# A sparse-attention and mixture kernel: the mixed tile goes to the end of a pair, value products and inverse spreads get fixed tiles, and the steps within a tile stand in another order

## The chip, the cores and the metric

The kernel runs on one core of a Trainium2 chip. The core has five engines with instruction streams of their own: TensorE (PE, with its weight loads shown apart as PEld), VectorE (DVE), ScalarE (ACT), GpSimd (POOL) and SyncE (SP), which issues the transfers. Each works through its stream in the order written; between the streams only semaphores set an order. The metric is the device time of one execution in microseconds (us); less is better.

## The reference

Attention with a threshold, then two feed-forward parts. Cut to the core:

```python
def _attn_ref(q, k, v, tau):             # q, k, v: (4, 8, 576, 64)
    scores = scale * np.matmul(q, k.transpose(0, 1, 3, 2))
    thresh = np.max(scores, axis=-1, keepdims=True) - tau
    scores = np.where(scores >= thresh, scores, -1000000000.0)
    scores = scores - np.max(scores, axis=-1, keepdims=True)
    attn = np.exp(scores)
    attn = attn / (np.sum(attn, axis=-1, keepdims=True) + 1e-09)
    return np.matmul(attn, v)
...
x = attn_out.transpose(0, 2, 1, 3).reshape(B * S, H * D)   # 2304 x 512
x = ((x @ w1) * (x @ w2)) @ w3 @ w_out
...  # gates P by 8 rounds of row and column scaling, then 8 experts:
for e in range(E):
    out += P[:, e:e + 1] * (np.maximum(x @ w1[e], 0.0) @ w2[e])
```

## The kernel before

The 32 heads are taken as 16 pairs. A pair has 9 tiles of 128 query rows: four of each head, and one **mixed tile** that holds the last 64 rows of both heads. TILES gives their order within a pair; the mixed tile `(None, 4)` stands fifth. Tiles are counted through from 0 to 143 (s), and the main loop of `attention` runs once for each s; below, t is s within its pair (0 to 8), and "step s" is one turn of the loop.

A tile goes through these operations, most of them spread over several turns:

- `scores` (PE, L158): four products of 288 columns, high and low part of k, into one of two PSUM buffers `s`. The mixed tile needs eight. Turn s makes the scores of tile s + 2.
- `rowmax` (DVE, L163), `thresh` and `expo` (ACT, L166, L171), also for tile s + 2 in turn s.
- `mask` (DVE, L178), for tile s in turn s: it compares with the threshold, multiplies and sums, and with its end the buffer `s` of that tile is free. As there are two buffers, the scores of tile s + 2 wait for the mask of tile s.
- `transp` (PE, L203) and `evac` (ACT, L208), for tile s - 1: four transposes into the only PSUM buffer `t`, then the copy to SBUF.
- for each group of three tiles `tails` (PE, L214) and `tail_out` (ACT, L219): the last 65 columns, transposed; also `flags`, `sums` (POOL) and `inverse` (DVE, L197).
- `pv` (PE, L251): the value products, in five units of a pair (two tiles each, the mixed tile alone in the last), 20 products a unit; UNITS says at which tile which unit is made.
- `repeat` (POOL), `spread` (PE, L285), `spread_out` (ACT, L293) and `x_out` (DVE, L304): twice in a pair (halves j = 0 and 1) the inverse sums are spread over the partitions by a transpose, copied to SBUF, and multiplied into the value products. `due` says at which turn.
- `vsum` (PE, L227): once in a pair, sums of v with a matrix of ones; its result is row 64 of v's last chunk.

`tails`, `spread` and `vsum` share one PSUM buffer, `tt`, so that each waits until ACT has copied out the one before it. The same turns carry the preparation of the next pair's q and k (`prep`, at turns given by PREP) and a second job, `W34`: it converts weights to float32 in four pieces (DVE L520, L523, L526, L528, with ACT and POOL; CONVERT says how many pieces in a turn) and multiplies w3 by w_out (L491; PRODUCTS says how many products in a turn).

The order within a turn, on all engines, is that of the string ORDER, one letter for each operation: m mask, S scores, T transp, q tails, e evac, l tail_out, V spread, o spread_out, i inverse, I repeat, f the copy of a finished product of W34, g flags, s sums, r and R preparation, c and z conversion, x rowmax, t thresh, X expo, y x_out, v value products, w products of W34.

After the last tile the mixture part (class `Moe`) follows, products of 384 and 512 columns on PE almost alone.

Of the kernel before, what the change touches and what calls it, by code (L numbers as in the profile page):

```python
# [36 lines left out]
PREP = {1: (0, 4), 2: (2, 1), 4: (3, 5), 5: (6,), 6: (7,), 7: (8,), 8: (9,)}  # L37
# [32 lines left out]
def attention(k):  # L70
# [204 lines left out]
    def spread(s):  # L275
        if (nj := due(s, 4, 8)) is None:
            return
# [3 lines left out]
        for u in ((0, 1), (2, 3, 4))[j]:  # L281
            a = 9 * (n % 2) + 4
# [56 lines left out]
    def groups(f, d):  # L339
# [5 lines left out]
        "T": tiles(transp, 1), "e": tiles(evac, 1), "g": groups(flags, 1), "s": groups(sums, 3), "i": groups(inverse, 5),  # L345
        "q": groups(tails, 3), "l": groups(tail_out, 3), "v": tiles(pv, 5),
# [662 lines left out]
```

## Time and profile before

| | |
|---|---|
| median of 3 runs | 2338.98 us (2338.29 to 2341.54) |
| the profiled execution | 2340.93 us |
| its span, first to last instruction | 2339.2 us |
| PE busy | 2198.3 us, 94% |
| DVE busy | 1259.5 us, 54% |
| ACT busy | 966.1 us, 41% |
| POOL busy | 1071.2 us, 46% |

The busy shares are means over two very different parts. In the attention part, up to some 506 us, no engine is full; from 525 us on PE is. So what the change is worth is to be read from the attention part alone: from which wait ends last in each turn. Times in the rows are microseconds from the start of the span, mean durations are nanoseconds.

### The profile page before, as it was taken

The page shows a single profiled execution, that of the slowest core. Times are in us where ns is not written, and L with a number is a line of the kernel's source. Part 1 is how long each engine was busy: PE and PEld are TensorE (multiplying, and loading weights), DVE is VectorE, ACT ScalarE, POOL GpSimd, SP SyncE. Part 2 cuts the span into 40 slices and gives each one's busy share as a digit, 9 for nine tenths or more (in the row PEclk, how much of TensorE's full clock was granted, in tenths as well). Part 3 has the DMA queues.
Part 4 walks back from the last instruction along what each step waited for, and adds up shares of the span by engine and source line. Part 5 has one row for each costly group of instructions (what it writes and reads, how often), then busy time and mean ns, then how long its engine had stood idle before and what let it go on. Part 6 is the DMA issues. An engine that isn't in the chain of part 4 may idle for free.

```text
span 2339.2 us, 32191 instructions
## 1 busy us (share of the span) xinstructions
PE 2198.3 (94%) x12624; PEld 1964.4 (84%) x12624; DVE 1259.5 (54%) x2175; ACT 966.1 (41%) x1805; POOL 1071.2 (46%) x1029
## 2 busy tenths in 40 slices
PE   6778888789999999999999999999999999999999
PEld 5566666668898988899999999999999899999998
DVE  6777777765645456544444644444444644444444
ACT  5666767653312233333333433333333443333332
POOL 4555544557301244444445644444446544444441
PEclk8999999989999999999999999999999999999999
DMA  4333343226534312211221222112221222111211
GB/s 141 93 88 115 106 120 112 85 90 254 189 152 180 145 39 71 72 61 66 73 73 60 76 91 73 70 57 73 72 72 55 100 72 72 55 72 72 72 58 51
DMA packets 57432, 213.39 MB, mean 91 GB/s; under 512 B 7104, under 2 KB 7104, under 8 KB 57280
## 3 DMA queue, kind: packets, MB, share of 16 engines
q1 hardware_dynamic: 57280, 211.33, 26.6%
q8 instruction: 99, 1.62, 0.3%
q14 instruction: 53, 0.43, 0.1%
HBM read 185.61 MB, written 25.69 MB: 90 GB/s over the span
## 4 chain that ended last, share of the span: by engine, by line
PE 67%; DVE 1%; issue 0%; ACT 0%; POOL 0%; DVEq 0%; ACTq 0%
PE ye L753 35%; PE py L683 18%; PE px L683 14%; DVE xl L672 0%; PE py L832 0%; DVE c L727 0%; PE px L832 0%; DVE c L738 0%; DVE prob L870 0%; ACT xh L671 0%; DVE acc L807 0%; POOL w1l L627 0%; DVE hl L749 0%; POOL w1l L624 0%; DVE small L867 0%
## 5 line engine op out<-in xcount | busy, mean ns | idle before, releaser
L753 PE MATMUL ye<-w2h,hl 128*128 128x512 f32 x1152 | 451.2, 392 | 0.0
L753 PE MATMUL ye<-w2h,hh 128*128 128x512 f32 x1152 | 451.1, 392 | 0.0
L753 PE MATMUL ye<-w2l,hh 128*128 128x512 f32 x1152 | 450.8, 391 | 0.0
L748 ACT ACTIVATE hh<-c 128x384 fp32r<-128x384 f32 x288 | 151.4, 526 | 611.1 <-DVE c L727 611.0
L629 POOL TENSOR_TENSOR w1l<-wt,w1h 128x1024 fp32r<-128x1024 f32 x104 | 252.6, 2428 | 285.1 <-ACT w1h L626 284.6
L683 PE MATMUL py<-xh,w1h 128*128 128x384 f32 x960 | 322.9, 336 | 7.6 <-DVE c L727 3.6
L683 PE MATMUL py<-xl,w1h 128*128 128x384 f32 x960 | 322.8, 336 | 3.4 <-DVE xl L672 3.4
L683 PE MATMUL py<-xh,w1l 128*128 128x384 f32 x960 | 322.1, 336 | 0.4 <-POOL w1l L629 0.4
L624 POOL TENSOR_TENSOR w1l<-raw,w1h 128x256 fp32r<-128x256 f32 x104 | 79.2, 761 | 480.1 <-ACT w1h L618 480.1
L683 PE MATMUL px<-xh,w1h 128*128 128x384 f32 x720 | 243.0, 337 | 5.5 <-ACT p L707 2.8
L683 PE MATMUL px<-xl,w1h 128*128 128x384 f32 x720 | 242.5, 337 | 2.7 <-DVE xl L672 2.7
L753 PEld LDWEIGHTS ye<-w2l,hh 128*128 128x128 f32 x1152 | 216.3, 188 | 32.6
L753 PEld LDWEIGHTS ye<-w2h,hl 128*128 128x128 f32 x1152 | 216.2, 188 | 32.6
L683 PE MATMUL px<-xh,w1l 128*128 128x384 f32 x720 | 242.0, 336 | 0.0
L753 PEld LDWEIGHTS ye<-w2h,hh 128*128 128x128 f32 x1152 | 216.3, 188 | 24.6 <-ACT x L779 0.2
L683 PEld LDWEIGHTS py<-xh,w1h 128*128 128x128 f32 x960 | 180.2, 188 | 31.3 <-DVE c L727 6.4
L683 PEld LDWEIGHTS py<-xl,w1h 128*128 128x128 f32 x960 | 180.2, 188 | 22.2 <-DVE xl L672 5.3
L158 PE MATMUL s<-kh,qs 128*128 128x288 f32 x320 | 106.9, 348 | 91.1 <-DVE p L178 84.0
L710 DVE TENSOR_TENSOR u<-py,p 128x384 f32<-128x384 f32 x120 | 66.8, 557 | 218.3 <-PE py L683 214.0
L683 PEld LDWEIGHTS py<-xh,w1l 128*128 128x128 f32 x960 | 180.1, 188 | 0.8 <-POOL w1l L629 0.8
L617 POOL TENSOR_TENSOR wt<-raw 128x512 f32<-128x512 f32 x104 | 139.0, 1336 | 74.9 <-DMA raw<-in_e 61.1
L749 DVE SCALAR_TENSOR_TENSOR hl<-c,hh 128x384 fp32r<-128x384 f32 x288 | 165.2, 574 | 9.3
(142 smaller groups left out, 4187.7 us busy)
## 6 DMA issues: line engine op xcount, KB each, us to landing
raw<-in_e SPq DMA_DIRECT2D x192, 512.0 KB, 4.0
r<-in_qk SPq DMA_DIRECT2D x60, 288.0 KB, 5.7
wraw<-in_w SPq DMA_DIRECT2D x32, 512.0 KB, 3.8
w1h<-w_kept SPq DMA_DIRECT2D x16, 896.0 KB, 5.1
w1l<-w_kept SPq DMA_DIRECT2D x16, 896.0 KB, 7.0
w_kept<-w1h SPq DMA_DIRECT2D x8, 896.0 KB, 7.4
w_kept<-w1l SPq DMA_DIRECT2D x8, 896.0 KB, 8.7
raw<-w SPq DMA_DIRECT2D x12, 512.0 KB, 3.7
```

Of the source, the lines that this page charges most:

```text
L158: nc.tensor.matmul(ps[:, c, 0:288], lhsT=qs[:, q0:q0 + 128], rhs=kk[:, h, cols], start=i == 0, stop=i == len(ops) - 1)
L617: nc.gpsimd.tensor_tensor(out=t[:, 0:2], in0=raw[:, 1:3], in1=raw[:, 0:2], op=ALU.subtract)
L624: nc.gpsimd.tensor_tensor(out=wl[:, 0], in0=raw[:, 0], in1=f32(wh[:, 0]), op=ALU.subtract)
L629: nc.gpsimd.tensor_tensor(out=wl[:, 3:7], in0=t, in1=f32(wh[:, 3:7]), op=ALU.subtract)
L683: self.nc.tensor.matmul(out, lhsT=w[:, wi, o], rhs=x[xi][:, d], start=n == 0 and not adds, stop=n == 5, skip_group_check=True)
L710: tt(out=self.u2, in0=py, in1=self.p1, op=ALU.add)
L748: nc.scalar.activation(hi, src, AF.Relu)
L749: self.later.append(lambda: nc.vector.scalar_tensor_tensor(out=lo, in0=src, scalar=0.0, in1=f32(hi), op0=ALU.max, op1=ALU.subtract))
L753: self.queue.append((out.shape[-1], lambda: self.nc.tensor.matmul(out, lhsT=l, rhs=r, start=start, stop=stop, skip_group_check=True)))
```

## The change

ORDER is another string: `T`, the transposes of tile s - 1, now stands ahead of `m` and `S`, the mask of tile s and the scores of tile s + 2; the leftover conversions `z` come right behind the mask, and `l` and `R` later. The mixed tile is the last of its pair. The value products have fixed turns, counted from the start of their pair: 5, 7, 9, 11, and 12 for the mixed tile (before: 7 and 8, 10, 11 and 13 for pair 0; 6, 8, 10, 11 and 13 for the others, with the mixed tile third). The spreads of the two halves stand at turns 8 and 11 (before 9 and 13), `repeat` at 7 and 10 (8 and 11), `x_out` at 8 and 13 (9 and 14), `inverse` one turn earlier. `vsum` is made one turn earlier (t = 1), the load of v two turns earlier (t = 4). The last chunk of v, which held the same 64 rows twice, holds them once and then zeros, and `vsum` uses all 128 rows of it. CONVERT, PRODUCTS and PREP have other numbers with the same sum of conversions over two pairs (20) and 29 products in place of 30.

```diff
-CONVERT = (1, 1, 1, 1, 1, 1, 1, 1, 0, 1, 1, 2, 2, 1, 1, 2, 1, 1)
-PRODUCTS = (0, 1, 0, 1, 4, 0, 4, 2, 1, 1, 3, 1, 0, 3, 0, 3, 3, 3)
-ORDER = "mSTqelVoiIfgsrRcxtXyvwz"
+CONVERT = (1, 0, 1, 1, 1, 2, 1, 1, 1, 1, 1, 1, 1, 1, 2, 2, 1, 1)
+PRODUCTS = (0, 4, 0, 0, 4, 0, 1, 0, 5, 0, 3, 0, 1, 4, 0, 2, 1, 4)
+ORDER = "TfmzeiSVsqIovgrcxRltXyw"
...
-UNITS = ({2: (0,), 3: (1,), 5: (4,), 6: (2,), 8: (3,)}, {1: (0,), 3: (1,), 5: (4,), 6: (2,), 8: (3,)})
+UNITS = {5: (0,), 7: (1,), 9: (2,), 11: (3,), 12: (4,)}
+AFTER = {'I': (7, 10), 'V': (8, 11), 'o': (8, 11), 'y': (8, 13)}
+SUMS_AT, VALUES_AT = 1, 4
...
         for i in range(5):
-            r = 128 if i < 4 else 64
-            nc.tensor.matmul(ps[0:65, 0:128], lhsT=last[0:r], rhs=rv[0:r, :, i], start=i == 0, stop=i == 4)
+            nc.tensor.matmul(ps[0:65, 0:128], lhsT=last, rhs=rv[:, :, i], start=i == 0, stop=i == 4)
...
-        n, t = divmod(s, 9)
-        for u in UNITS[min(n, 1)].get(t, ()):
+        for n, u in ((n, u) for n in (s // 9 - 1, s // 9) if 0 <= n < NP for u in UNITS.get(s - 9 * n, ())):
...
-    def due(s, first, second):
-
-        s -= 5
-        n, t = divmod(s, 9)
-        if t == first and 0 <= n < NP:
-            return n, 0
-        if t == second - 9 and 0 < n <= NP:
-            return n - 1, 1
-        if t == second and 0 <= n < NP:
-            return n, 1
+    def due(s, what):
+
+        for n in (s // 9 - 1, s // 9):
+            for j in range(2):
+                if 0 <= n < NP and s - 9 * n == AFTER[what][j]:
+                    return n, j
         return None
```

PE at the start of pair 8 before: the scores of tile 74, the transposes of tile 71, the tails `tt23` of its group, and the spread `rb7_0` of pair 7, first half.

```order
L158 MATMUL s74_2890<-kl8_2581,qs8_2579 128x288
L203 MATMUL t71_2895<-ident_83,p23_2765 128x128 x4
L214 MATMUL tt23_2900<-ident_83,p23_2765 65x128 x3
L285 MATMUL rb7_0_2908<-ident_83,rw7_0_2861 128x128 x2
L158 MATMUL s75_2928<-kh8_2580,qs8_2579 128x288
```

The spread stood right behind the tails, in the same buffer. Now that of pair 8 stands a turn earlier in its pair, at t = 8, PE again:

```order
L160 MATMUL s82_3223<-kl9_2930,qs9_2928 128x288
L281 MATMUL rb8_0_3228<-ident_83,rw8_0_3187 128x128 x2
L487 MATMUL w34_3_2970<-woh_108,w3h19_2805 128x512
L487 MATMUL w34_3_2970<-wol_109,w3h19_2805 128x512
L487 MATMUL w34_3_2970<-woh_108,w3l19_2806 128x512
L487 MATMUL w34_3_2970<-woh_108,w3h20_2933 128x512
L205 MATMUL t80_3243<-ident_83,p26_3143 128x128 x4
L160 MATMUL s83_3259<-kh9_2929,qs9_2928 128x288
```

No tails are in that turn, and the transposes of tile 80 stand ahead of the scores of tile 83. The second place is PE at t = 4 of pair 8 before: the end of a value product of pair 7, four products of W34, the next scores.

```order
L251 MATMUL pv7_1_2960<-pt71_2904,rv7_2463 64x128
L251 MATMUL pv7_1_2960<-ptt23_2906,rv7_2463 64x128 x2
L491 MATMUL w34_3_2884<-woh_108,w3l19_2814 128x512
L491 MATMUL w34_3_2884<-woh_108,w3h19_2813 128x512
L491 MATMUL w34_3_2884<-wol_109,w3h19_2813 128x512
L491 MATMUL w34_3_2884<-woh_108,w3l19_2814 128x512
L158 MATMUL s79_3104<-kh8_2580,qs8_2579 128x288
```

Now, PE at the same t, behind the scores of tile 78:

```order
L160 MATMUL s78_3069<-kl8_2572,qs8_2570 128x288
L487 MATMUL w34_3_2970<-wol_109,w3h19_2805 128x512
L487 MATMUL w34_3_2970<-woh_108,w3l19_2806 128x512
L487 MATMUL w34_3_2970<-woh_108,w3h19_2805 128x512
L487 MATMUL w34_3_2970<-wol_109,w3h19_2805 128x512
L205 MATMUL t76_3101<-ident_83,p25_3026 128x128 x4
L160 MATMUL s79_3109<-kh8_2571,qs8_2570 128x288
```

The value products have gone to the turns on either side; the four products of W34 have that turn for themselves.

## Rows read from the trace of the kernel before

**Rows 1.** Stretches: length; PE, PEld, DVE, ACT, POOL busy (instructions); PE clock; DMA share, GB/s.
```profile
12.00:506.00 494.00, 392.35 (x3312) 326.91 (x3312) 366.88 (x730) 336.30 (x724) 252.53 (x371) 0.94 0.35 101
525.00:2339.00 1814.00, 1790.21 (x9205) 1624.14 (x9203) 875.98 (x1425) 613.35 (x1052) 801.09 (x636) 1.00 0.24 87
291.90:296.90 5.00, 2.60 (x17) 2.00 (x17) 2.78 (x8) 3.17 (x8) 0.19 (x1) 1.00 0.00 0
297.10:300.40 3.30, 3.30 (x29) 2.74 (x28) 2.31 (x7) 2.08 (x5) 0.67 (x4) 0.50 0.57 150
```
**Rows 2.** Waits, 30 to 500 us: who for whom, us in total, times, longest.
```profile
DVE nmx L163 <- PE s L158: 86.0, 101, 2.4
...
DVE x L304 <- ACT xo L293: 24.8, 15, 1.7
...
DVE p L178 <- ACT e L171: 1.2, 3, 0.5
```
**Rows 3.** Timeline of DVE in pairs 8 and 9: start, length, instruction.
```profile
260.29 0.81 DVE L178 SCALAR_TENSOR_TENSOR p<-s,thr,e 128x576 f32<-128x576 f32 x1
...
282.15 0.81 DVE L178 SCALAR_TENSOR_TENSOR p<-s,thr,e 128x576 f32<-128x576 f32 x1
...
283.86 0.76 DVE L163 TENSOR_REDUCE nmx<-s 128x1 f32<-128x576 f32 x1 [0.30 <-PE s L158]
284.54 0.81 DVE L178 SCALAR_TENSOR_TENSOR p<-s,thr,e 128x576 f32<-128x576 f32 x1
...
321.94 0.80 DVE L178 SCALAR_TENSOR_TENSOR p<-s,thr,e 128x576 f32<-128x576 f32 x1
```
**Rows 4.** Timeline of all engines in the first turn of pair 9.
```profile
291.24 0.82 DVE L178 SCALAR_TENSOR_TENSOR p<-s,thr,e 128x576 f32<-128x576 f32 x1
...
293.89 0.48 ACT L219 ACTIVATE ptt<-tt 65x384 f32<-65x384 f32 x1
294.51 0.41 PE L285 MATMUL rb<-ident,rw 128*128 128x128 f32 x2 [0.82 <-ACT ptt L219]
...
294.96 0.38 ACT L293 ACTIVATE xo<-rb 128x256 f32<-128x256 f32 x1 [0.59 <-PE rb L285]
...
295.38 0.42 DVE L304 TENSOR_TENSOR x<-pv,xo 128x256 f32<-128x256 f32 x1 [1.65 <-ACT xo L293]
295.72 0.81 DVE L178 SCALAR_TENSOR_TENSOR p<-s,thr,e 128x576 f32<-128x576 f32 x1
```
**Rows 5.** Timeline of PE in pair 8, at the full clock.
```profile
261.45 0.39 PE L491 MATMUL w<-wol,w3h 128*128 128x512 f32 x1
261.68 0.39 PE L491 MATMUL w<-woh,w3l 128*128 128x512 f32 x1
...
269.99 0.29 PE L158 MATMUL s<-kh,qs 128*128 128x288 f32 x1
...
271.04 0.60 PE L203 MATMUL t<-ident,p 128*128 128x128 f32 x4
271.57 1.09 PE L251 MATMUL pv<-pt,rv 128*64 128x128 f32 x16
...
272.82 1.45 PE L227 MATMUL vs<-rv,last 128*65 128x128 f32 x10
274.20 0.40 PE L158 MATMUL s<-kh,qs 128*128 128x288 f32 x1
...
274.83 0.60 PE L203 MATMUL t<-ident,p 128*128 128x128 f32 x4
275.27 0.49 PE L214 MATMUL tt<-ident,p 128*65 128x128 f32 x3
```
**Rows 6.** Groups of DVE, 30 to 500 us: busy us, mean ns, idle before.
```profile
L523 DVE SCALAR_TENSOR_TENSOR cva<-wraw,cva 128x512 int32<-128x512 int32 x38 | 31.0, 815 | 0.0
...
L528 DVE TENSOR_SCALAR cvs<-cvq 128x512 int32<-128x512 int32 x39 | 21.9, 561 | 0.5
```
**Rows 7.** Loads of q and k (L104), 0 to 40 us, issue to landing.
```profile
DMA to landing us min/median/max: 2.8/3.9/9.3
```

More of the change, by code (lines that the diff above doesn't have):

```diff
@@ L42 @@
 CHUNKS = "oowoooo33o3o33ww3ww3333wwww3w33w3ww3ww3w"
-TILES = (((0, 0), (0, 1), (1, 0), (1, 1), (None, 4), (0, 2), (1, 2), (0, 3), (1, 3)),
-         ((0, 0), (1, 0), (0, 1), (1, 1), (None, 4), (0, 2), (1, 2), (0, 3), (1, 3)))
-UNITS = ({2: (0,), 3: (1,), 5: (4,), 6: (2,), 8: (3,)}, {1: (0,), 3: (1,), 5: (4,), 6: (2,), 8: (3,)})
+TILES = (((0, 0), (0, 1), (1, 0), (1, 1), (0, 2), (1, 2), (0, 3), (1, 3), (None, 4)),
+         ((0, 0), (1, 0), (0, 1), (1, 1), (0, 2), (1, 2), (0, 3), (1, 3), (None, 4)))
+UNITS = {5: (0,), 7: (1,), 9: (2,), 11: (3,), 12: (4,)}
+AFTER = {'I': (7, 10), 'V': (8, 11), 'o': (8, 11), 'y': (8, 13)}
+SUMS_AT, VALUES_AT = 1, 4
 def tile_of(n, t):
@@ L57, in tiles_of @@
     if u == 4:
-        return 4, 4
+        return 8, 8
     return tuple(TILES[min(n, 1)].index((h, u)) for h in range(2))
@@ L252, in pv @@
                                      start=i == 0, stop=i == 4)
-    def due(s, first, second):
-        s -= 5
-        n, t = divmod(s, 9)
-        if t == first and 0 <= n < NP:
-            return n, 0
-        if t == second - 9 and 0 < n <= NP:
-            return n - 1, 1
-        if t == second and 0 <= n < NP:
-            return n, 1
+    def due(s, what):
[3 more added lines that the diff above has]
+                    return n, j
         return None
     def repeat(s):
-        if (nj := due(s, 3, 6)) is None:
+        if (nj := due(s, "I")) is None:
             return
         n, j = nj
-        a = 9 * (n % 2) + 5 * j
+        a = 9 * (n % 2) + 4 * j
         r = rin[:, a:a + 4].rearrange("p (h u) -> p u h" if n + j == 0 else "p (u h) -> p u h", u=2)
@@ L275, in spread @@
     def spread(s):
-        if (nj := due(s, 4, 8)) is None:
+        if (nj := due(s, "V")) is None:
             return
@@ L281, in spread @@
         for u in ((0, 1), (2, 3, 4))[j]:
-            a = 9 * (n % 2) + 4
+            a = 9 * (n % 2) + 8
             c = 128 * (u % 2) if u < 4 else 256
@@ L288, in spread_out @@
     def spread_out(s):
-        if (nj := due(s, 4, 8)) is None:
+        if (nj := due(s, "o")) is None:
             return
@@ L298, in x_out @@
     def x_out(s):
-        if (nj := due(s, 4, 9)) is None:
+        if (nj := due(s, "y")) is None:
             return
@@ L344, in attention @@
         "m": tiles(mask, 0), "S": tiles(scores, -2), "x": tiles(rowmax, -2), "t": tiles(thresh, -2), "X": tiles(expo, -2),
-        "T": tiles(transp, 1), "e": tiles(evac, 1), "g": groups(flags, 1), "s": groups(sums, 3), "i": groups(inverse, 5),
-        "q": groups(tails, 3), "l": groups(tail_out, 3), "v": tiles(pv, 5),
+        "T": tiles(transp, 1), "e": tiles(evac, 1), "g": groups(flags, 1), "s": groups(sums, 3), "i": groups(inverse, 4),
+        "q": groups(tails, 3), "l": groups(tail_out, 3), "v": pv,
         "V": spread, "I": repeat, "o": spread_out, "y": x_out, "f": lambda s: fill.out(),
@@ L373, in attention @@
             load(n + 2, t // 2 - 1)
-        if n < NP and t == 2:
-            vsum(n)
-        if n < NP and t == 6:
+        if (s - SUMS_AT) % 9 == 0 and 0 <= s - SUMS_AT < NT:
+            vsum((s - SUMS_AT) // 9)
+        if n < NP and t == VALUES_AT:
             load_v(n + 1)
@@ L974, in _layouts @@
     v = pairs(inputs["v"])
-    vv = c(np.concatenate([v[:, :, :512].reshape(NP, 2, 4, 128, D), np.concatenate([v[:, :, 512:]] * 2, axis=2)[:, :, None]],
+    vv = c(np.concatenate([v[:, :, :512].reshape(NP, 2, 4, 128, D), np.concatenate([v[:, :, 512:], np.zeros_like(v[:, :, 512:])], axis=2)[:, :, None]],
                           axis=2).transpose(0, 3, 1, 2, 4))
```

2 lines of the change are left out of this document (1 added, 1 removed).

## The prediction

> **What bounds the kernel now.** I read the stretches first [rows 1]. From 525 us to the end PE is busy 1790 of 1814 us at the full clock; the change doesn't touch that part, which only begins sooner or later. In the attention part, 12 to 506 us, no engine is full: PE 392 of 494 us, DVE 367, ACT 336. So something is waited for in turn, and the waits say what [rows 2]: DVE's row maximum waits 86.0 us for the scores, and x_out 24.8 us for the copied spread, while the mask hardly ever waits for the exponential (1.2 us). The ring is: mask of tile s on DVE, which frees the buffer; scores of tile s + 2 on PE; row maximum on DVE; the next mask. PE comes late to it, though it is idle a fifth of the time: its work is heaped.
>
> The pace: from the mask of tile 72 to that of tile 90, 18 turns or two pairs, it is 321.94 - 260.29 = 61.65 us [rows 3], 3.43 us a turn. A turn in which nobody is late takes 284.54 - 282.15 = 2.39 us [rows 3], of which 0.67 is the maximum and 0.73 the mask.
>
> **Unit prices**, from the distance of starts at the full clock [rows 5]: scores of a mixed tile 271.04 - 269.99 = 1.05, of another half of it, 0.53; transposes 274.83 to 275.27 = 0.44; tails three quarters of that, 0.33; a spread 0.22 (two transposes) or 0.33 (three); a value product unit 271.57 to 272.82 = 1.25; the sums of v 272.82 to 274.20 = 1.38; a product of W34 0.23. The unit of the mixed tile, with 64 columns, has no row at the full clock: between 0.6 (half the columns) and 1.25, and I take 1.0, since as many instructions are issued. On DVE a piece of the conversion takes 0.56 to 0.82 [rows 6], less the 0.08 by which records overlap (283.86 + 0.76 against 284.54) [rows 3].
>
> **The old order, as a check of the count.** For each turn I take the larger of what PE and what DVE has in it. DVE: 1.40 for mask and maximum, and what stands between them, at least 0.99 (scores must get through; 1.51 for the mixed tile); x_out and pieces behind the maximum are added. PE: scores, transposes and all that stands in that turn.
> - t = 0 is set by neither, but by a chain through four engines [rows 4]: tails, their copy on ACT (0.48, from 293.89), only then the spread on PE (294.51, after 0.82 of idling), its copy (294.96), x_out (295.38, for which DVE idled 1.65), mask at 295.72. From mask to mask 4.48.
> - t = 2 is the worst heap: mixed scores, transposes, a value unit, sums of v: 1.05 + 0.44 + 1.25 + 1.38 = 4.12. At t = 4, scores, transposes, spread, value unit and four products: 3.47. At t = 6, tails in place of the spread: 3.47. At t = 3, 5 and 7 PE has 0.97 to 1.5 to do, and DVE sets 2.39, 2.79 and 2.39.
> - The nine turns of pair 8: 4.48 + 2.39 + 4.12 + 2.39 + 3.47 + 2.79 + 3.47 + 2.39 + 2.45 = 27.95. Pair 9 in the same way 29.36. Together 57.3; measured 61.65, so 4.35 is in no term: the clock (below), and lateness that goes from turn to turn.
>
> **The new order**, by the same count:
> - The chain of t = 0 goes. The spread of the first half now stands at t = 8, where no tails are; its buffer was emptied two turns earlier. Behind scores, spread 0.22 and copy 0.38 run beside the maximum (0.76), so x_out finds its input there. At t = 0 PE has scores 0.53, tails 0.33, a value unit 1.25, transposes 0.44: 2.55.
> - Each turn now has one heap at most: t = 1 four products and the sums of v, 0.53 + 0.92 + 1.25 + 0.44 = 3.14; t = 2 spread and value unit 2.55; t = 3 tails and mixed unit 2.30; t = 4 four products 1.89; t = 5 and 7 a value unit 2.22; t = 6 mixed scores, tails, one product 2.05; t = 8 spread and four products 2.11. The sums of v are taken at 1.25 without the switch to 64 rows (bounds 1.0 and 1.38).
> - DVE: 2.39 where it holds a piece or less between mask and maximum; with more (t = 4, 5, 7) 2.57 to 2.65; 2.91 for the mixed tile; x_out, 0.42 long and 0.34 from start to start [rows 4], adds 0.40 at t = 4 and t = 8.
> - The larger of both: 2.55 + 3.14 + 2.55 + 2.39 + 2.97 + 2.65 + 2.91 + 2.57 + 2.79 = 24.5, and for the next pair, with more pieces of conversion, 25.2: together 49.7.
>
> DVE's own need over two pairs is nearly the same, 48.2 before and 47.8 now, and PE's 43 and 42: no work is saved. What goes is that the two are at their worst in different turns.
>
> To 49.7 I add what the count will miss again. Before it was 4.35; I take 3.6, somewhat less, because part of it is the clock, and keep 0 and 4.35 as ends. That gives 53.3, a gain of 8.35 for two pairs. The first pair runs in, with other waits, so I count 15 pairs: 15 x 4.18 = 63 us; the ends are 15 x 3.80 = 57 (with 4.35) and 15 x 5.98 = 90.
>
> **Smaller parts.** The first preparation of pair 1's k is asked for one turn earlier, at the start, and ACT then waits for a load that may take up to 9.3 us to land [rows 7], with thresholds queued behind it; one turn later there was no such wait, so it costs 0 to 5 us, one of the slow first turns; I take 2. At the end some seven more products of W34 come behind the last scores, 7 x 0.23 = 1.6 us of PE, with their store behind it on SP: 0 to 4, taken 1. Repeat on POOL now leads the spread by one turn in both halves: the copy and a conversion ahead of it still end within the turn, cost nothing, and up to 0.5 a pair if POOL is late. v's load is as large as before, and SP reaches it a turn after the last reader of that buffer: nothing.
>
> Sum: 63 - 3 = 60. The profiled execution took 2340.9 us, which is 2 above the median of the runs, so 2281 for such a run and **2279** as a median.
>
> **The clock.** In the first turn of pair 9, where the chain leaves PE 2.60 us of work in 5.00, the clock is still full; right behind it, from 297.10, it is at 0.50 of full, 1.2 in place of 2.4 GHz, for 3.3 us [rows 1]. It falls so about once in a pair, and over the part it is 0.94. PE needs twice its time there, so it loses up to 1.65 us a pair. With the chain gone the new order has no such stretch of waiting, and I expect a clock near 1.0.
>
> The Trainium skill, "TensorE: Matmul & The Clock Gate", part 4 (PE-mode transpose), says that the full clock doesn't engage for transposes. By it the falls could stay, at turns of little but scores and transposes, and the time would be that of rival 1; the rows here don't tell transposes from products in that, so it has only that rival's chance.
>
> **Rivals.**
> 1. *The clock goes on falling once a pair*, then most likely at t = 6. For it: the turn ahead of the old fall held scores, transposes, tails and a spread and waiting, and t = 6 holds scores, transposes, tails and one product. Against: PE doesn't wait there for a chain. Price: up to 1.65 x 15 = 25 us more than forecast: 2304.
> 2. *DVE becomes the bound alone.* PE's early transposes let every score start at once, and t = 1 and 2 are made up for in the light turns. Then 47.8 for two pairs, and the gain is 15 x 6.9 = 104, less 3: about 2238. For it: DVE's waits for scores are 86 us now. Against: nothing in a ring of four engines meets its bound.
> 3. *Scores wait behind transposes: slower.* The transposes of tile s - 1 now stand ahead of the scores of tile s + 2, and need the only buffer `t` emptied by ACT, which comes to that after the exponential of tile s. If ACT runs late, PE stands at the transposes with the scores queued behind, and DVE waits for these. For it: in some turns a copied product, a conversion or w3's rounding stands ahead of that copy on ACT. Against: the mask waits for the exponential only 1.2 us in all [rows 2], so ACT has room now. It decides once ACT's copy ends later than PE's heap; beyond that each us is a us of that turn. The forecast gains 8.35 / 18 = 0.46 a turn; a copy that comes 0.6 too late in each of 135 turns takes that back and 0.14 more: 2339 + 135 x 0.14 + 3 = 2361.
> 4. *The heaps only change places*: PE at t = 0 to 2 is behind by 1.1 us and drags the next turns, and only the chain's gain is left, 4.48 less the mean of 2.55 and 2.80, 15 x 1.8 = 27, less 3: 2315. With rival 1 on top nothing is left: no change.
>
> **How the numbers follow.** Forecast 2262 to 2298: 0.60. Rival 1 around 2304: 0.13. Rival 2, 2238 to 2262: 0.10. Rival 3: 0.08, of which 0.06 ends slower. Rival 4: 0.09, of which 0.03 is no change. The range leaves out the lower half of rival 2, all of rival 3, and the upper part of rival 4: 2250 to 2312. What a measurement of this kernel can tell from no change is 0.2%, 4.7 us. Faster by more than that: 0.60 + 0.13 + 0.10 + 0.02 + 0.06 = 0.91; within it 0.03; slower 0.06.
>
> **What would show it.** Right: two pairs take some 53 us from mask to mask; x_out's 24.8 us of waiting near zero; the maximum's wait for scores well below 86 us; PE clock over the part above 0.97. Chain wrong: x_out still waits for the spread's copy. Heaps wrong: the scores still start over 1 us after the mask in some turns, at t = 2 and 3 first. Rival 3: PE idles at the transposes, released by the copy `pt` on ACT. The forecast is wrong as a whole if the attention part doesn't end 50 to 70 us sooner, or if the mixture part, 1814 us here, grows.

## The result: 2285.15 us, and where the time went

The changed kernel takes 2285.15 us (median of 4 runs, 2283.88 to 2288.12) against 2338.64 us for the kernel before beside it: a ratio of 0.9771, with a 95% interval of 0.9754 to 0.9788, 53.5 us less. Forecast were 2279, with 2250 to 2312 as range. Its profiled run has a span of 2281.8 us.

The stretches of the changed kernel that answer to [rows 1] (PE, PEld, DVE, ACT, POOL busy with their instructions; PE clock; DMA share, GB/s):

```profile
12.00:450.00 438.00, 367.89 (x3319) 309.14 (x3320) 382.41 (x734) 341.75 (x724) 259.55 (x374) 0.98 0.40 114
525.00:2281.00 1756.00, 1736.36 (x8902) 1573.44 (x8901) 844.91 (x1379) 593.57 (x1017) 758.30 (x604) 1.00 0.23 82
```

The attention part is what became shorter. Its last mask ends at 448.99 us, before at 506.79: 57.8 us sooner. From that mask to the end of the span it is 2281.8 - 449.0 = 1832.8 us, before 2339.2 - 506.8 = 1832.4. So nothing came from the mixture part, and nothing was given back there. In the attention part PE is busy 24 us less than before, though it has as many instructions: its clock is 0.98 in place of 0.94. DVE is busy 15 us *more* than before with as many instructions (382.41 against 366.88 in [rows 1]), in a stretch 56 us shorter: 87% of it in place of 74%.

The waits of the changed kernel, 30 to 460 us, that answer to [rows 2] (us in total, times, longest):

```profile
ACT thr L168 <- DVE nmx L165: 48.3, 67, 2.8
DVE nmx L165 <- PE s L160: 45.1, 61, 2.7
...
ACT pt L210 <- PE t L205: 15.5, 27, 2.0
...
PEld t L205 <- ACT pt L210: 4.3, 13, 1.2
...
DVE x L300 <- ACT xo L289: 0.7, 1, 0.7
```

The maximum waits 45.1 us for scores, not 86.0, and x_out, which waited 24.8 us for the copied spread, waits once, 0.7 us. ACT's thresholds now wait for DVE's maximum, 48.3 us in place of 2.5: DVE is the engine that others wait for.

The pace, answering to [rows 3]: the masks of tiles 72 and 90, and those of tiles 99, 117 and 135, start 18 turns, or two pairs, apart:

```profile
239.99 0.80 DVE L180 SCALAR_TENSOR_TENSOR p<-s,thr,e 128x576 f32<-128x576 f32 x1
...
294.12 0.80 DVE L180 SCALAR_TENSOR_TENSOR p<-s,thr,e 128x576 f32<-128x576 f32 x1
...
319.67 0.81 DVE L180 SCALAR_TENSOR_TENSOR p<-s,thr,e 128x576 f32<-128x576 f32 x1
...
372.79 0.81 DVE L180 SCALAR_TENSOR_TENSOR p<-s,thr,e 128x576 f32<-128x576 f32 x1
...
425.02 0.81 DVE L180 SCALAR_TENSOR_TENSOR p<-s,thr,e 128x576 f32<-128x576 f32 x1
```

That is 54.13 us for the tiles from which the prediction took 61.65, and later 53.12 and 52.23. The mean turns show where in the pair it was won. Each number here is the time from the end of the mask of tile t of a pair to the end of the next mask, averaged over the turns that end with the masks of tiles 20 to 139; the last column is the sum of the nine, a pair. The lower rows belong to the experiments.

| kernel | t=0 | 1 | 2 | 3 | 4 | 5 | 6 | 7 | 8 | pair |
|---|---|---|---|---|---|---|---|---|---|---|
| before | 4.79 | 2.61 | 3.82 | 4.13 | 2.49 | 3.77 | 2.97 | 3.44 | 2.65 | 30.68 |
| changed | 2.48 | 2.89 | 2.79 | 2.69 | 3.16 | 2.52 | 3.43 | 3.49 | 3.47 | 26.93 |
| counted for it, first of two pairs | 2.55 | 3.14 | 2.55 | 2.39 | 2.97 | 2.65 | 2.91 | 2.57 | 2.79 | 24.52 |
| e1, before with the spread later | 2.72 | 3.79 | 3.94 | 3.79 | 2.49 | 3.76 | 2.95 | 3.35 | 2.66 | 29.45 |
| e3, spread on the tails' turn | 3.81 | 3.13 | 3.12 | 2.69 | 3.19 | 2.52 | 3.59 | 3.50 | 3.14 | 28.69 |
| e4, scores first | 2.56 | 3.02 | 2.80 | 3.01 | 3.12 | 2.95 | 3.83 | 3.56 | 3.79 | 28.64 |
| e5, kl twice | 2.54 | 3.02 | 2.80 | 2.71 | 3.50 | 2.53 | 3.98 | 3.95 | 3.62 | 28.65 |
| e6, qs at t = 1 and 2 | 2.55 | 2.91 | 3.75 | 2.40 | 3.20 | 2.52 | 3.48 | 2.72 | 2.85 | 26.38 |
| e7, conversion shifted | 2.43 | 2.84 | 2.89 | 3.00 | 4.61 | 2.70 | 3.67 | 3.73 | 2.84 | 28.70 |
| e9, qs at t = 0 and 1 | 2.88 | 2.70 | 2.64 | 2.75 | 3.17 | 2.51 | 3.41 | 2.75 | 2.87 | 25.67 |
| e10, sums of v at t = 2 | 2.52 | 3.07 | 2.38 | 3.78 | 3.04 | 2.50 | 3.45 | 3.55 | 3.47 | 27.76 |

t = 0, the turn of the chain, gives 2.3 us, t = 2, 3 and 5, in which PE came late, give 3.7. But t = 4 and t = 6 to 8 have grown by 2.0 together, and t = 1 by 0.3. What stands there is DVE's. This is DVE at t = 7 (the masks bound the turn):

```profile
366.44 0.81 DVE L180 SCALAR_TENSOR_TENSOR p<-s,thr,e 128x576 f32<-128x576 f32 x1
367.17 0.08 DVE L180 DVE_READ_ACCUMULATOR p<-s,thr,e 128x1 f32 x1
367.17 0.17 DVE L199 RECIPROCAL rin<-ssum 128x3 f32<-128x3 f32 x1
367.37 1.36 DVE L133 SCALAR_TENSOR_TENSOR qs<-r,qs 64x288 fp32r<-64x288 f32 x1
368.76 0.51 DVE L516 TENSOR_SCALAR cva<-wraw 128x512 int32<-128x512 int32 x1
369.19 0.74 DVE L165 TENSOR_REDUCE nmx<-s 128x1 f32<-128x576 f32 x1
369.86 0.80 DVE L180 SCALAR_TENSOR_TENSOR p<-s,thr,e 128x576 f32<-128x576 f32 x1
...
370.70 0.46 DVE L133 SCALAR_TENSOR_TENSOR qs<-r,qs 64x288 fp32r<-64x288 f32 x1
```

DVE doesn't idle once here. The same qs instruction takes 1.36 us, and 0.46 one turn later. The difference is POOL, at the same time:

```profile
367.12 1.29 POOL L526 TENSOR_TENSOR wf<-cvl,cvq 128x512 f32<-128x512 f32 x1
368.36 0.63 POOL L269 COPY rw<-rin 128x256 f32<-128x256 f32 x1
```

POOL began 0.25 us before qs and ended at 368.41; qs ended at 368.73, that is 0.32 after it. So it is for all of DVE's instructions between 44 and 449 us: qs takes 0.46 in each of the 16 cases in which no POOL tensor instruction overlaps it, and 0.45 to 1.51 in the other 41; the second piece of the conversion (L519) 0.68 to 0.70 in 17 and 0.69 to 1.67 in 20. The maximum and the mask, which read PSUM, take 0.74 to 0.76 and 0.80 to 0.81 either way. e5 tests this.

### The profile page after: what moved, and what is told of

It reads as the page before. It is cut to its first block, busy times and chain, and to the rows that moved or that the text cites. A ratio compares the mean times of both kernels' runs of the same rounds, so it can differ in the third digit from the quotient of the medians.

```text
span 2281.8 us, 32262 instructions
## 1 busy us (share of the span) xinstructions
PE 2171.4 (95%) x12624; PEld 1945.2 (85%) x12624; DVE 1272.9 (56%) x2175; ACT 971.9 (43%) x1805; POOL 1074.0 (47%) x1029
## 4 chain that ended last, share of the span: by engine, by line
PE 69%; DVE 1%; issue 0%; ACT 0%; POOL 0%; DVEq 0%; ACTq 0%
PE ye L749 36%; PE py L679 19%; PE px L679 14%; DVE xl L668 0%; PE py L828 0%; DVE c L723 0%; PE px L828 0%; DVE c L734 0%; DVE prob L866 0%; ACT xh L667 0%; DVE acc L803 0%; POOL w1l L623 0%; DVE hl L745 0%; POOL w1l L620 0%; DVE small L863 0%
```

## The experiments

The theory to be tested: three things gave the gain, the chain at t = 0, the heaps taken apart, and transposes done while PE waits; and what kept it from being larger is DVE, which is full at t = 4 and 6 to 8 and is held up there by POOL. All medians are of 4 runs, of 5 in e12; the kernel before took 2338.84 us beside e1 to e4, 2339.97 beside e5 to e8, 2340.30 beside e9 to e11, 2341.38 beside e12, and 2338.64 beside the changed kernel. So a distance between an experiment and the changed kernel is good to some 2 to 3 us, and the turns of the traces say more than the medians.

**e1: the chain alone, taken from the kernel before.**

```diff
-        if (nj := due(s, 4, 8)) is None:      # spread and spread_out
+        if (nj := due(s, 5, 8)) is None:
-        if (nj := due(s, 4, 9)) is None:      # x_out
+        if (nj := due(s, 5, 9)) is None:
```

> The kernel before with one edit: the spread of a pair's first half, its copy and x_out stand at t = 1 of the next pair and no longer at t = 0, where the tails are. It asks what the chain of t = 0 was worth by itself. Theory (the chain is a term of its own): t = 0 and t = 1 together took 4.79 + 2.61 = 7.40 us on average in the trace of before; without the chain t = 0 should take some 2.6 and t = 1, with spread and x_out, some 3.0, so 1.8 a pair, 27 us in all: about 2312. If the falls of the clock go with it, up to 1.65 a pair more: down to 2287. Rival (the chain only hid the heap at t = 2, which now stands out): 0 to 10 us gained, 2329 to 2339.

Measured: 2324.04 us, ratio 0.9940 (0.9921 to 0.9960), 14.8 us gained, between what the theory and the rival gave. t = 0 fell by 2.07 us, more than expected, but t = 1 grew by 1.18, to 3.79 in place of 3.0. The waits, 30 to 487 us, show why:

```profile
DVE nmx L163 <- PE s L158: 71.9, 94, 2.1
...
PEld pv L251 <- DVE x L304: 27.6, 15, 1.9
...
PE pv L251 <- DVE x L304: 24.0, 15, 1.6
...
DVE x L304 <- ACT xo L293: 14.7, 15, 1.0
```

The value unit of the mixed tile, at t = 1, writes the buffer that x_out empties, so it now waits up to 1.6 us for an x_out that comes a turn later, 15 times; the kernel before has no such wait. So moved alone, the chain for the most part changes its place: the change gave the value units new places with it. The clock is at 0.97 over 12 to 487 us. Between the ninth and the last mask it falls 4 times, in the kernel before 15 times, and that is where most of the gain lies: without a fall, pair 7 of the kernel before takes 29.27 us, and pairs 7, 9, 11 and 13 here take 29.00 to 29.11; with one, pairs 9, 11 and 13 of the kernel before take 30.69 to 30.82. What a fall costs is worked out further below.

**e2 and e3: the chain put back into the changed kernel.** e2 only changes the order inside the turn, so that tails and their copy stand ahead of the spread, which e3 needs.

```diff
-ORDER = "TfmzeiSVsqIovgrcxRltXyw"
+ORDER = "TfmzeiSsqlVIovgrcxRtXyw"
```

> The changed kernel with another order inside a turn: tails and their copy stand ahead of the spread (behind the sums on POOL) in place of behind it. No step changes its turn. It is there as the ground for the run that puts the spread on the tails' turn, which needs this order. Theory: within 5 us of the changed kernel, 2280 to 2290, since no turn has both tails and a spread except t = 2 and t = 8, which have spreads and no tails. Rival (order on ACT decides: the tails' copy now stands ahead of the thresholds and exponentials): 0.3 us in three turns of a pair, some 14 us slower, 2299.

Measured: 2287.68 us, ratio 0.9780 (0.9765 to 0.9795): as the theory has it, no difference that can be told from the changed kernel. e3 is e2 and:

```diff
-UNITS = {5: (0,), 7: (1,), 9: (2,), 11: (3,), 12: (4,)}
-AFTER = {'I': (7, 10), 'V': (8, 11), 'o': (8, 11), 'y': (8, 13)}
-SUMS_AT, VALUES_AT = 1, 4
+UNITS = {5: (0,), 7: (1,), 10: (2,), 11: (3,), 12: (4,)}
+AFTER = {'I': (7, 10), 'V': (9, 11), 'o': (9, 11), 'y': (9, 13)}
+SUMS_AT, VALUES_AT = 0, 4
```

> The changed kernel with the order of e2, and the spread of the first half, its copy and x_out put back to t = 0 of the next pair, on the turn of the tails. The value unit of that turn goes to t = 1 and the sums of v come from t = 1 to t = 0, so that t = 1 keeps 3.14 us of PE work. It asks whether the chain costs in the new order what it cost in the old. Theory: t = 0 grows from 2.48 to about 4.3 us, 1.8 a pair, 27 us over e2: about 2312; if the clock falls again behind the chain once in a pair, up to 25 more, 2337, and the granted clock over the part drops from 0.98 to about 0.94. Rival (DVE is nearly full in the new order, so that PE's lateness is made up in other turns): under 8 us over e2, and a clock of 0.98.

Measured: 2315.37 us, ratio 0.9901 (0.9884 to 0.9918), 27.7 us over e2, where the theory had 27 without the clock. t = 0 grows from 2.48 to 3.81, by 1.3 and not by 1.8, and x_out's wait is back, once a pair (e3, 30 to 480 us):

```profile
DVE nmx L165 <- PE s L160: 59.3, 68, 2.7
DVE x L300 <- ACT xo L289: 15.2, 15, 1.6
```

The clock over 12 to 480 us is 0.95: between the ninth and the last mask it falls 8 times, in e2 3 times. So the theory's number came out of two parts. Pairs 7, 11, 12 and 13, in which the clock falls in neither run, take 1.4 us more than in e2 (28.98 and 27.57 in pair 11), which makes some 21 us in 15 pairs: that is the chain. And where the clock falls right behind the chain, in pairs 8, 10 and 14, t = 1 takes 3.99 to 4.31 us, against 2.67 in the others from pair 4 on: 1.3 to 1.6 us for each fall. The rival falls: DVE being nearly full didn't hide the chain.

**e4: scores ahead of the transposes.**

```diff
-ORDER = "TfmzeiSVsqIovgrcxRltXyw"
+ORDER = "fmzSTeiVsqIovgrcxRltXyw"
```

> The changed kernel with one edit in the order of a turn: the transposes of tile s - 1 stand behind the scores of tile s + 2 and no longer ahead of everything else in the turn. Theory: PE does these 0.44 us of transposes while it waits for the mask; behind the scores they come on top in the turns in which PE is late, t = 1 to 3 (the row maximum waits 0.84, 0.92 and 0.38 us for the scores there): 3 x 0.44 x 16 = 21 us slower, 2306, and the turns 6 to 8 keep their 3.47. Rival A (scores come sooner, because they no longer wait for the transposes): faster, 2270 to 2283. Rival B (the ring levels it out): within 4 us of 2285.

Measured: 2310.65 us, ratio 0.9881 (0.9860 to 0.9902), 25.5 us slower. The price is the theory's (21), but the place isn't: t = 1 and 2 grew by 0.14 together, t = 3, 5, 6 and 8 by 0.32 to 0.43 each. What happens is seen at t = 5 of one pair and the start of t = 6, with all that DVE, ACT and POOL do there left out but this:

```profile
329.01 0.60 ACT L210 ACTIVATE pt<-t 128x512 f32<-128x512 f32 x1 [0.61 <-PE t L205]
...
330.62 0.67 ACT L129 ACTIVATE qs<-r 128x576 fp32r<-128x576 f32 x1
...
331.33 0.46 DVE L133 SCALAR_TENSOR_TENSOR qs<-r,qs 64x288 fp32r<-64x288 f32 x1 [0.77 <-ACT qs L129]
...
333.24 1.41 POOL L140 TENSOR_TENSOR kl<-r,kh 128x576 fp32r<-128x576 f32 x1 [2.33 <-ACT kh L137]
...
333.83 1.38 DVE L522 SCALAR_TENSOR_TENSOR cvq<-cvq,cva 128x512 f32<-128x512 f32 x1
```

The transposes come late, ACT stands at their copy (109.7 us of such waits over the part, 15.5 in the changed kernel), the copies behind it on ACT are late, DVE waits 0.77 us for one of them, and POOL's kl, late as well, now lies beside a piece of the conversion, which takes 1.38 us; at that turn of the changed kernel it took 0.88. DVE waits 7.8 us more for scores over the part, which is less than a third of the loss; for ACT it waits 6.3 us at t = 3, 5 and 8 from tile 72 on, where in the changed kernel it doesn't. So the transposes in front are worth less for PE's 0.44 us than for an ACT that runs on time. The clock has a part in the 25.5 us too: it falls 10 times between the ninth and the last mask, in the changed kernel twice. Pairs 11 to 14, without a fall in either, are 1.1 us longer on average, some 17 us in 15 pairs.

**e5: POOL's work doubled at two places.**

```diff
-            (nc.gpsimd if n or h else nc.vector).tensor_tensor(out=kl[:, h], ...)
+            for _ in range(2 if n else 1):
+                (nc.gpsimd if n or h else nc.vector).tensor_tensor(out=kl[:, h], ...)
```

> The changed kernel with POOL's subtraction for kl issued twice for every pair but the first (the second writes the same values again): 1.42 us more of POOL twice in a pair, at t = 3 and t = 6; no other engine gets an instruction more. POOL is busy 240 of 404 us in the part of the changed kernel from 44.68 to 448.99 us, so it has room. Theory (DVE operations that read and write SBUF stand still while POOL works beside them; in the changed kernel those without overlap take 0.46 or 0.69 us, those with it up to 1.5 to 1.7): DVE's busy time grows though it has the same instructions, and at t = 6 and 7, where DVE is full, the time with it: 0.5 to 1.4 us a pair, 8 to 21 us slower, 2293 to 2306; the row maximum and the mask, which read PSUM, stay at 0.75 and 0.81 us. Rival (the long durations are of another origin, and POOL has room): within 3 us of 2285.

Measured: 2309.25 us, ratio 0.9865 (0.9851 to 0.9880), 24 us slower, a little over the theory's upper bound. First the groups of DVE in the changed kernel, 44 to 449 us (busy us, mean ns, idle before), then those of e5 over the same turns, to 474 us, where the line numbers behind the edit are one higher:

```profile
L165 DVE TENSOR_REDUCE nmx<-s 128x1 f32<-128x576 f32 x134 | 100.8, 753 | 44.5 <-PE s L160 44.2
L133 DVE SCALAR_TENSOR_TENSOR qs<-r,qs 64x288 fp32r<-64x288 f32 x57 | 39.8, 699 | 1.8
...
L516 DVE TENSOR_SCALAR cva<-wraw 128x512 int32<-128x512 int32 x36 | 23.5, 652 | 0.7
L524 DVE TENSOR_SCALAR cvs<-cvq 128x512 int32<-128x512 int32 x37 | 20.7, 559 | 1.2
```

```profile
L166 DVE TENSOR_REDUCE nmx<-s 128x1 f32<-128x576 f32 x135 | 101.5, 752 | 41.3 <-PE s L161 41.1
L133 DVE SCALAR_TENSOR_TENSOR qs<-r,qs 64x288 fp32r<-64x288 f32 x57 | 50.1, 878 | 1.8
...
L525 DVE TENSOR_SCALAR cvs<-cvq 128x512 int32<-128x512 int32 x37 | 31.2, 844 | 1.2
L517 DVE TENSOR_SCALAR cva<-wraw 128x512 int32<-128x512 int32 x37 | 26.3, 711 | 0.7
```

qs grew from 699 to 878 ns and the last piece of the conversion from 559 to 844, though DVE got no instruction more, and POOL, busy 240 of 404 us in the changed kernel, had room for its own. The maximum stayed at 752. With the two groups not shown the five grew by 28.5 us, about the loss. The clock falls 7 times here and twice in the changed kernel, but pairs 10 to 14, without a fall in either, are 1.0 to 1.4 us longer, some 19 us in 15 pairs. This is the theory, and the rival is out. The Trainium skill, "SBUF — State Buffer", section "Who interferes with whom", says that VectorE and GpSimd share one pair of SBUF ports, that an instruction of VectorE with two SBUF inputs, beside one of GpSimd that reads SBUF, or in a two-port mode, waits until GpSimd's has ended where that was issued first, and that one with at most one SBUF input outside these modes doesn't. The runs agree with it on all that they show: the row at 367.37, and the maximum and the mask, which read the scores from PSUM.

**e6 to e9: work moved out of the full turns.** e6 moves the last two quarters of qs from t = 7 and 8 to the turns in which DVE waits for scores. Here tile 3 of a pair is scored ahead of the last quarter's correction, so that its scores read that quarter uncorrected (e8 too); the instructions are the same.

```diff
-PREP = {..., 6: (7,), 7: (8,), 8: (9,)}
+PREP = {..., 6: (7,), 10: (8,), 11: (9,)}
     def parts(s, which):
-        n, t = divmod(s, 9)
-        for part in PREP.get(t, ())[which]:
-            prep(n + 1, part)
+        for n, t in (divmod(s, 9), (s // 9 - 1, s % 9 + 9)):
+            for part in PREP.get(t, ())[which] if n >= 0 else ():
+                prep(n + 1, part)
```

> The changed kernel with the last two quarters of qs on DVE moved from t = 7 and 8 of the pair before to t = 1 and 2 of the pair that uses them (for every pair but the first), ahead of the scores that need them. The row maximum waits 1.04 and 0.78 us for the scores in those turns, and nothing at t = 6 to 8. Theory (DVE is the bound of the turns 4 and 6 to 8, and PE that of 1 to 3): t = 7 and t = 8 fall from 3.49 and 3.47 to some 2.9, t = 1 and 2 stay at 2.79, so 1.2 us a pair, 18 us: 2267, with 2255 to 2272 as bounds (the operations taken away are 0.46 us long alone and up to 1.4 beside POOL). Rival (turns 7 and 8 are set by PE or by ACT and DVE is only late with them): 2280 to 2290.

Measured: 2274.99 us, ratio 0.9719 (0.9702 to 0.9735), 10 us gained, short of the theory's 13 to 30. t = 7 and 8 fell to 2.72 and 2.85, as the theory has it, but t = 2 grew to 3.75: there the moved quarter and the conversion came beside POOL.

e7 moves pieces of the conversion instead:

```diff
-CONVERT = (1, 0, 1, 1, 1, 2, 1, 1, 1, 1, 1, 1, 1, 1, 2, 2, 1, 1)
+CONVERT = (1, 1, 2, 1, 1, 2, 1, 0, 0, 1, 1, 2, 1, 1, 2, 2, 1, 0)
```

> The changed kernel with another list of how many pieces of the conversion each turn holds: none at t = 8, one fewer at t = 7 of the first of two pairs, more at t = 1 and 2 (and with it other pieces in other turns). The number over two pairs stays 20. Theory (as in e6): three pieces of 0.42 to 0.69 us, up to 1.7 beside POOL, leave full turns, so 0.6 to 1.5 us a pair: 2262 to 2276. Rival (PE or ACT sets these turns): 2280 to 2290. Against the theory speaks that the pieces that POOL and ACT have with a conversion move too and can stretch DVE in another place.

Measured: 2312.78 us, ratio 0.9880 (0.9865 to 0.9894), 28 us *slower*: neither theory nor rival. t = 8 fell to 2.84 as meant, but t = 4 grew from 3.16 to 4.61. The pieces moved against qs and kl. In the trace of e7, 44 to 472 us:

```profile
L165 DVE TENSOR_REDUCE nmx<-s 128x1 f32<-128x576 f32 x134 | 101.1, 755 | 54.8 <-PE s L160 54.5
L133 DVE SCALAR_TENSOR_TENSOR qs<-r,qs 64x288 fp32r<-64x288 f32 x57 | 48.1, 843 | 1.8
```

qs takes 843 ns on average in place of 699, and the maximum waits 10 us more for scores; the clock is back at 0.96 over the part. At t = 4 the pieces and quarters that stand there would take 1.01 us alone in both kernels; here they take 2.29, in the changed kernel 1.17. Some 5 us of the 28 come behind the last mask. Between the ninth and the last mask the clock falls 10 times, not twice; what that costs here, and how the rest divides, stays open. What was wrong in my theory: a piece is not worth its 0.42 to 0.69 us but what POOL makes of it in its new place.

e8 is e6 with a milder shift of the conversion:

```diff
+CONVERT = (1, 1, 1, 1, 1, 2, 1, 1, 0, 1, 1, 2, 1, 1, 2, 2, 1, 0)
```

> The changed kernel with the edit of e6 and, beside it, a milder shift of the conversion: none at t = 8, one each at t = 1 of the first pair and one more at t = 2 of the second. Theory: the gain of e6 and some 0.4 us a pair more, 2255 to 2265, until DVE has no full turn but t = 4 and 6. Rival (once t = 7 and 8 are lighter, PE's heaps at t = 1 to 3 set the time): no better than e6.

Measured: 2286.57 us, ratio 0.9771 (0.9747 to 0.9795): 11.6 us worse than e6. t = 8 is at 2.90, t = 3 grew to 3.49. The rival has the sign, but not the cause: at t = 1 to 3 DVE is busy 2.8, 3.2 and 3.2 us of turns of 2.9, 3.4 and 3.5, and waits 0.4 us for scores in the three together, so it is again DVE and not PE's heaps.

e9 repairs e6: the quarters go to t = 1 and t = 0, the last one ahead of tile 3's scores, and t = 2 keeps its work.

```diff
+PREP = {..., 6: (7,), 9: (9,), 10: (8,)}
```

> The changed kernel with the last two quarters of qs on DVE moved from t = 7 and 8 to t = 1 and 0 of the pair that uses them (for every pair but the first): both stand ahead of every score that reads them. In e6 the quarter that stood at t = 2 met POOL's conversion and the turn grew from 2.79 to 3.75 us; here t = 2 keeps its work, and at t = 0 POOL is busy for 0.8 us only. Theory (full DVE turns, stretched by POOL): t = 7 and 8 fall to 2.7 and 2.9 us as in e6, t = 0 grows by 0.3 to 0.5, t = 1 stays below 2.95: 0.7 to 1.1 us a pair, 2268 to 2275. Rival (the phase of the conversion against POOL decides more than the place of qs): 2276 to 2290.

Measured: 2267.19 us (2266.04 to 2269.44), ratio 0.9688 (0.9671 to 0.9705): 18 us below the changed kernel, better than the theory's 2268 to 2275, and the fastest here. In its trace, over 12 to 433 us and 30 to 433 us:

```profile
12.00:433.00 421.00, 365.40 (x3317) 307.18 (x3318) 385.33 (x733) 340.36 (x724) 257.06 (x374) 0.98 0.42 119
```

```profile
DVE nmx L165 <- PE s L160: 25.4, 46, 2.4
```

DVE's busy time has not fallen (385.33 against 382.41). What fell is its waiting for scores, from 45.1 to 25.4 us: 20 us of work now lies in turns in which DVE stood idle.

**e10: one heap put back.**

```diff
-SUMS_AT, VALUES_AT = 1, 4
+SUMS_AT, VALUES_AT = 2, 4
```

> The changed kernel with one number changed: the sums of v stand at t = 2 in place of t = 1. PE's work is the same; t = 2 becomes a heap again, scores, transposes, the spread of three, a value unit and the sums, 0.53 + 0.44 + 0.33 + 1.25 + 1.25 = 3.80, and t = 1 has only 1.89 left. Theory (a turn takes the larger of what PE and DVE have in it): t = 1 falls from 2.89 to some 2.5, t = 2 grows from 2.79 to 3.8, so 0.6 us a pair, 9 us slower: 2294. Rival (PE's lateness in one turn is made up in the next, so heaps don't matter as long as the sum is the same): 2282 to 2288.

Measured: 2299.20 us, ratio 0.9821 (0.9806 to 0.9836), 14 us slower with the same work: heaps cost, and the rival is out. In pairs 9, 10, 11, 13 and 14, without a fall of the clock, it is 0.5 to 0.75 us a pair, the theory's 0.6 or some 9 us in all; two more falls of the clock are in the rest. My places were off by one turn: the sums stand at the end of a turn's code, so that the scores behind them belong to the next turn, and t = 3 grew from 2.69 to 3.78 while t = 2 fell to 2.38.

**e11: the start.**

```diff
-        for part in PREP.get(t, ())[which]:
+        for part in ({0: (), 1: (0, 4)}.get(s) if s < 2 else PREP.get(t, ()))[which]:
```

> The changed kernel, with the first half of kh of the second pair prepared at t = 1 of the first pair in place of t = 0, that is as the kernel before did it there; all later pairs as changed. In the changed kernel ACT waits 6.3 us at this copy for a load, and the ninth mask ends at 44.68 us, against 43.01 before. Theory (the early copy costs the start of the attention part 1.7 us): 2283.5, and the ninth mask at 43.0. Rival (the wait only moves, since the load comes when it comes): 2285.

Measured: 2286.04 us, ratio 0.9769 (0.9752 to 0.9786): no difference. ACT's wait for the load shrinks from 6.3 to 0.7 us and the ninth mask ends at 43.77 in place of 44.68, but the last mask ends at 448.86 in place of 448.99. What is late at the start is made up for later.

**e12: 64 rows again.**

```diff
-            nc.tensor.matmul(ps[0:65, 0:128], lhsT=last, rhs=rv[:, :, i], start=i == 0, stop=i == 4)
+            r = 128 if i < 4 else 64
+            nc.tensor.matmul(ps[0:65, 0:128], lhsT=last[0:r], rhs=rv[0:r, :, i], start=i == 0, stop=i == 4)
```

> The changed kernel with one part undone: the last of the five steps of the sums of v reads 64 rows again in place of 128 zero-padded ones. In the trace of before the sums took 1.38 us from start to start, in that of the changed kernel 377.72 to 378.81, 1.09. They stand at t = 1, where the row maximum waits for PE. Theory (PE's time counts in full in a turn in which PE is late): 0.29 us in each of 15 pairs, 4.4 us slower: 2289.5. Rival (lateness of t = 1 is made up in the turns behind it): within 1.5 us of 2285.

Measured: 2289.64 us, which is the theory's number; but beside it the kernel before was slower too, and the ratio, 0.9780 (0.9766 to 0.9793), puts it only 2 us over the changed kernel, within its interval. The sums themselves are clear. In the changed kernel:

```profile
377.72 1.25 PE L228 MATMUL vs<-rv,last 128*65 128x128 f32 x10
378.81 0.60 PE L205 MATMUL t<-ident,p 128*128 128x128 f32 x4
```

and in e12:

```profile
358.55 1.39 PE L229 MATMUL vs<-rv,last 128*65 128x128 f32 x10
359.87 0.66 PE L205 MATMUL t<-ident,p 128*128 128x128 f32 x4
```

1.09 us against 1.32, and so in all 15 later pairs within 0.01. What it is worth the turns say. In the pairs without a fall of the clock t = 2, whose scores stand behind the sums, takes 0.31 us more than in the changed kernel (3.07 and 2.75 in pair 13), and the other eight turns differ by 0.02 at most on average. That is 4.6 us in 15 pairs: the theory, and the rival is out.

## Why the prediction was right, and where it was not

**The chain.** That it goes is right: one x_out waits, 0.7 us, and t = 0 fell by 2.31. The step that prices it at 1.8 us a pair, 27 in all, is less well borne out than e3's 27.7 us look: some 21 of them are the chain, 1.4 a pair, and the others come with falls of the clock, which the 27 didn't hold. That the two sums agree is luck.

**The heaps.** Right that they cost, wrong in their places. The count puts what PE does behind the scores (value products, sums of v, products of W34) in its own turn, but it delays the scores of the next one, as e10 and e12 show for the sums. So the old heaps of t = 2, 4 and 6 show a turn later: before, t = 3, 5 and 7 take 4.13, 3.77 and 3.44 us, where the count of pair 8 has 2.39, 2.79 and 2.39, and t = 4 and 6 take 2.49 and 2.97, where it has 3.47. What saved the forecast is that it uses the sums of nine turns, which came nearer: 28.65 us a pair counted, 30.68 measured, of which some 1.3 are the clock (below). t = 3 and 5 fell by 1.44 and 1.25; t = 2 fell by 1.03, but there the clock counts too (below). e10, which restores one heap of the old kind, costs 14 us, 9 of them without the clock. The parts undone one at a time, 27.7 + 25.5 + 14 us, come to more than the 53.5 gained. In all three the clock falls again, 8, 10 and 4 times; by the pairs without a fall they are some 21, 17 and 9 us.

**The count, and the 3.6 us added to it.** Two pairs were forecast at 53.3 and take 53.12 and 52.23 in the late part, 53.9 on average. But the working holds two errors that met, and that they cancelled is luck. The first is the term for DVE's pieces. From [rows 6] I took 0.56 to 0.82 us each, whatever their turn, and so counted 8.27 us for t = 6 to 8 of the first of two pairs; over both kinds of pair they take 10.39. These prices are means over pieces that take 0.42 to 0.69 alone and, before, up to 1.8 beside POOL. The trace of before held the spread that would have told so, and I read only the means. The second is the cause of the 4.35 us that the old count missed: I put it down to the clock and to dragged lateness, expected a small part of it to go, and kept 3.6. The clock alone was 2.4 to 3.0 of it (below), and that went almost wholly. What the new count misses is DVE's stretching in good part: a pair takes 26.93 us and was counted at 24.85 (24.5 and 25.2), 2.1 less, and even if all by which the second of two pairs was counted longer lay at t = 6 to 8, these three would be at 8.6 in the count and exceed it by 1.8. So the surplus stayed for another reason than the one given.

**No work saved.** "DVE's own need over two pairs is nearly the same": its instructions are, its time isn't. Over the 135 turns from the ninth mask to the last it was busy 341.36 us before and is 354.58 now, since the work that stood beside idle time now meets POOL. That is 13 us of DVE's time given back. Its quarters of qs and pieces of the conversion, some 106 us if each took its time alone, took 131 us before and take 148 now.

**The clock.** Right: 0.98 over the part, above the 0.97 asked for. From 94 us on, in the third pair, it doesn't fall again until behind the last mask:

```profile
94.00:455.00 361.00, 308.16 (x2866) 259.55 (x2864) 316.25 (x608) 286.36 (x608) 215.43 (x312) 1.00 0.38 110
```

These are turns of scores, transposes, tails and products, and the trace agrees in them with the forecast and not with rival 1. The Trainium skill's sentence that the full clock doesn't engage for transposes ("TensorE: Matmul & The Clock Gate", part 4) doesn't decide here, where no turn holds transposes alone.

What the falls cost before is in the trace of before too. Here are t = 1 and 2 together in pair 7, where the clock didn't fall behind the chain, and in pair 9, where it did:

```profile
236.42:242.26 5.84, 5.77 (x64) 5.07 (x65) 5.24 (x14) 4.67 (x11) 2.35 (x6) 1.00 0.65 170
296.53:303.86 7.33, 7.27 (x64) 6.30 (x65) 5.15 (x13) 5.18 (x12) 3.35 (x7) 0.77 0.60 153
```

PE has 64 instructions in both, is busy nearly from end to end, and takes 1.50 us longer for them. In the even pairs these two turns take 6.40 to 6.54 us with a fall and 5.28 to 5.30 without one. So a fall costs some 1.2 to 1.5 us, near the 1.65 of the prediction. From the ninth mask to the last the clock fell 15 times before and falls twice now: 13 falls at 1.2 to 1.5 are 16 to 20 us of the 53.5, an estimate. The prediction has this term, but only as a part of the 0.75 us by which it lowered the 4.35 of two pairs, 5.6 us in all.

**Small parts.** The start was taken at 2 us; the ninth mask is 1.7 later, and by e11 nothing of it reaches the end. The end was taken at 1 and is 0.4. The unit of the mixed tile was taken at 1.0; it is 0.73 (382.89 to 383.62 on PE), and the trace of before had a row for it at the full clock after all, in pair 7 (237.65 to 238.38, 0.73 too). The sums are 1.09 for 1.25.

**Rivals.** 1 falls with the clock at 0.98, 4 with t = 3 and 5 and with e10. 3 didn't happen: PE waits 4.3 us in all for the copy at its transposes, and e4, the order without that risk, is slower, because the risk of a late ACT lay on the other side. 2 didn't happen as told, but its mechanism is the state the kernel has come to: DVE is full in four of nine turns, and PE's lateness decides less.

**The 6 us missed.** Forecast was 63 for the pace, less 3. From the ninth mask to the last it is 463.78 us before and 404.31 now, 59.5 in place of 63; the start takes 1.7 and the end 0.4 of it. Against the 2281 us forecast for a profiled run, the profiled 2283.88 is 2.9 us off; the other 3.3 us lie in the step from that run to the median.

## What to carry to other kernels

When a ring of engines loses time in no one place, count each turn for each engine and see whether their worst turns coincide; moving heaps apart then gains without saving any work, and one heap put back shows whether the count is right. Before taking a mean duration from a group of instructions, look at its shortest and longest, and at what the other engines did: an instruction with two durations can hide a wait that the profile doesn't list. Before calling a difference the price of an edit, count the falls of the clock in both traces and compare pairs without one. Moving work into idle turns pays only if the engine that can stop it is not at work there: the quarters of qs paid 18 us, the same idea with the conversion cost 28.

## What the runs showed of the hardware that I had not expected

DVE's quarters of qs and pieces of the conversion, all on SBUF data, stand still when they begin beside a running tensor instruction of POOL, until about its end, and then take nearly their full time; the profile counts the whole as busy. Only where POOL had 0.09 to 0.16 us left (16 cases between 44 and 449 us) do they still take their own time. Here is one of the longest cases in the changed kernel, DVE first, POOL behind it:

```profile
389.55 0.42 DVE L516 TENSOR_SCALAR cva<-wraw 128x512 int32<-128x512 int32 x1
390.00 1.67 DVE L519 SCALAR_TENSOR_TENSOR cva<-wraw,cva 128x512 int32<-128x512 int32 x1
```

```profile
389.64 1.48 POOL L526 TENSOR_TENSOR wf<-cvl,cvq 128x512 f32<-128x512 f32 x1
```

POOL's 389.64 + 1.48 is 391.12, and DVE's instruction ends at 391.67, 0.55 later. It is the same in all 76 stretched instructions between 44 and 449 us: qs ends 0.31 to 0.32 us behind a tensor instruction of POOL, the pieces that take 0.69 alone 0.55, and those that take 0.42 alone 0.28 to 0.29. It works the other way round too. POOL's L526 takes 1.34 to 1.49 us in the 21 cases in which it began while a qs or an L516 was still running, as here, and 1.28 to 1.29 in the other 16, beside DVE's maximum or mask as well. So DVE's busy share is no measure of its work when POOL is busy.

And five steps of the sums of v of which the last reads 64 rows take 0.23 us longer than five of 128 rows, more than a whole step of the latter, 1.09 / 5 = 0.22.
